# One 128-row product per pair of modes: a zero-padded block-diagonal stationary in place of two 64-row products

## The chip, the core and the metric

The kernel runs on one core of a Trainium2 chip. The metric is the device time of one execution in microseconds (us). Each kernel was executed several times; a median and the single runs are given. The profile is taken from one of those executions, and its "span" is some 1.7 us shorter than the time of the same run, so spans are compared with spans and times with times. Short names: PE is the matrix engine, PEld its weight loads, DVE the vector engine, ACT the scalar engine, POOL the engine that issues the weight loads from memory, DMA the sixteen transfer engines of the core.

## The reference

Attention features first (left out here), then a mixing of frequencies: for each of 64 modes, an eight-row matrix of complex numbers is multiplied with its own complex 512 x 512 matrix.

```python
# x: (8, 576, 512) out of a linear attention; w_r, w_i: (64, 512, 512) fp32; w_ch: (512, 512)
X  = np.fft.rfft(x, axis=1)
Xr, Xi = np.real(X[:, :64]), np.imag(X[:, :64])
Yr = einsum('bmd,mde->bme', Xr, w_r) - einsum('bmd,mde->bme', Xi, w_i)
Yi = einsum('bmd,mde->bme', Xr, w_i) + einsum('bmd,mde->bme', Xi, w_r)
y  = np.fft.irfft(Yr + 1j * Yi, n=576, axis=1)      # modes from 64 on are zero
u  = x + y
out = u + np.maximum(u @ w_ch, 0.0)
```

`w_r` and `w_i` together are 134 MB in fp32 and are used once. They are most of what the core reads.

## The kernel before

The modes are handled in 31 pairs and one last pair, whose second mode has a path of its own. The weights of a pair lie in one tile of 128 partitions: 64 for the even mode, 64 for the odd one, 16 blocks of 512 columns (`NDW = 16`). `NDC` is 4, `B` is 8, `D` is 512. A pair uses 32 products with 64 rows each, into two PSUM banks; four of them at a time stand side by side in four column tiles of the array, so a bank holds four partial results below one another. A copy brings a bank to SBUF, and four matmuls with a 0/1 table (`pick_sb`) sum the four parts and turn the result. The cut below is shortened: the `pin(...)` calls, which keep the program order, are left out, and a two-branch `if` is written in one line.

```python
def product(P, kk, w, dc):                                   # one of 32 per pair
    c = dc % NDC * 32                                        # column tile
    n = 32 if dc < NDC else 2 * B
    rows = slice(0, 128) if last else HALVES[kk % 2]         # 64 rows: even or odd mode
    nc.tensor.matmul(P[c : c + n, :], xt_cols(dc, kk, n), w[rows, dc, :],
                     start=(dc < NDC), stop=(dc >= n_dc - NDC), tile_position=(rows.start, c), ...)

def evacuate(kk, P):                                         # one per mode
    st = ystage.tile([128, D], F16, tag="ystage", bufs=2, ...)
    nc.vector.tensor_copy(out=st, in_=P) if kk % 2 == 0 else nc.scalar.copy(out=st, in_=P)
    return st

def picks(kk, st):                                           # four per mode
    for ec in range(NDC):
        nc.tensor.matmul(yt_ps[:, ec, kk % 8, :], st[:, ec * 128 : ec * 128 + 128], pick_sb)

def mode_pair(p):
    w = w_get(p)                                             # issues the next load into the buffer that is free
    ...
    for dc in range(NDW):
        for P, kk in zip(Ps, kks):
            product(P, kk, w, dc)
    sts = [evacuate(kk, P) for P, kk in zip(Ps, kks)]
    work_slot(p, "mid")                                      # other work of the program, spread over the pairs
    for kk, st in zip(kks, sts):
        picks(kk, st)
    ...
    # (cut: copies of yt_ps, further work, filler matmuls)
```

## Time and profile before

| | before |
|---|---|
| time, three runs | 423.23, 423.29, 424.82 us; median 423.29 |
| profiled span | 420.7 us |
| instructions counted | 8570 |
| PE busy | 292.1 us (69%), 3714 matmuls and as many weight loads |
| DVE, ACT, POOL busy | 215.7, 163.5, 56.9 us |

A share of busy time tells little here: no compute engine is above 69%, but the row of the DMA engines stands at 9 tenths for nearly the whole span. How the rows are read is told in the prediction, which shows them. One part of the page it does not show is the list of DMA queues (columns: number and kind, packets, MB, share of the sixteen engines' time). Two of its lines carry no data at all. They matter later, so here they are for the kernel before:

```profile
q8 instruction: 29, 0.48, 0.4%
q14 instruction: 8, 0.07, 0.0%
```

These queues bring the engines their instructions. Each of the 29 packets of the first is about 0.48 MB / 29 = 16 KB.

### The profile page before, as it was taken

What the parts mean: (1) busy time and instruction counts of PE and PEld (TensorE: products, weight loads), DVE (VectorE), ACT (ScalarE), POOL (GpSimd) and SP (SyncE); (2) the same over time, 40 slices, a digit from 0 to 9 for tenths busy, and PEclk for the clock granted to TensorE, in tenths of its full rate; (3) what the DMA queues carried; (4) which work ended last, traced back from release to release, by engine and by line L of the source; (5) the groups of instructions that cost most, each with busy time, mean ns of one, the idle gap of its engine ahead of it and who ended that gap; (6) DMA issues with size and microseconds to landing.
All of it is one profiled execution on the core that took longest, in us unless ns stands there. A gap on an engine that the chain in (4) does not pass through costs nothing.

```text
span 420.7 us, 8570 instructions
## 1 busy us (share of the span) xinstructions
PE 292.1 (69%) x3714; PEld 162.7 (39%) x3714; DVE 215.7 (51%) x446; ACT 163.5 (39%) x269; POOL 56.9 (14%) x99
## 2 busy tenths in 40 slices
PE   1369997999617645444343686978789896999992
PEld 0257775877402322122122232433334332365420
DVE  4588899695203453354544433454335332422794
ACT  4677797854202102000000243444335351231782
POOL 4222224210101111111111111111111111130000
PEclk9999998589855555555555589899989896899997
DMA  8999999999999999999999999999999999997697
GB/s 219 211 212 216 210 217 209 226 217 209 225 213 224 211 210 221 218 209 221 217 210 221 217 206 223 220 206 221 221 206 221 222 206 220 223 204 154 234 395 320
DMA packets 16421, 93.24 MB, mean 222 GB/s; under 512 B 2048, under 2 KB 2944, under 8 KB 11968
## 3 DMA queue, kind: packets, MB, share of 16 engines
q0 software_dynamic: 12416, 81.47, 93.1%
q1 hardware_dynamic: 3968, 11.22, 7.1%
q8 instruction: 29, 0.48, 0.4%
q14 instruction: 8, 0.07, 0.0%
HBM read 163.93 MB, written 9.44 MB: 412 GB/s over the span
## 4 chain that ended last, share of the span: by engine, by line
DMA 64%; PE 22%; DVE 6%; issue 2%; POOL 2%; ACT 2%; DVEq 0%; POOLq 0%; ACTq 0%
DMA w<-in_moe_w_i_dram 51%; DMA pick_sb<-row_pick 8%; PE P L438 7%; DMA k<-in_k_dram 5%; PE acc L732 3%; PE acc L771 2%; PE kvp L259 2%; POOL w L119 2%; PE zl L421 1%; PE eps L673 1%; ACT ke L210 1%; DVE ys L448 1%; DVE x L295 1%; PE ya L650 1%; PE yt L456 1%
## 5 line engine op out<-in xcount | busy, mean ns | idle before, releaser
L438 PE MATMUL P<-w,xt_c 64*32 64x512 bf16 (+2 forms) x1000 | 51.0, 538 | 59.5 <-DMA w<-in_moe_w_i_dram 58.1
L448 DVE CAST ys<-P 128x512 f16<-128x512 f32 x32 | 22.1, 692 | 123.7 <-PE P L438 123.7
L450 ACT CAST ys<-P 128x512 f16<-128x512 f32 x31 | 18.1, 585 | 155.6 <-PE P L438 155.6
L119 POOL DMA_DIRECT2D w<-in_moe_w_r_dram x31 | 17.3, 557 | 247.4 <-PE P L438 97.4
L438 PEld LDWEIGHTS <-xt_c 64*32 64x32 bf16 (+2 forms) x1000 | 16.8, 128 | 79.9 <-DMA w<-in_moe_w_i_dram 43.4
L673 PE MATMUL eps<-wch,xTw 128*128 128x512 f16 x144 | 39.4, 400 | 0.0
L165 PEld LDWEIGHTS <-qT 64*128 64x128 f16 (+1 forms) x640 | 23.4, 124 | 31.6 <-issue 18.0
L259 PE MATMUL kvp<-vpad,ke 32*128 32x130 f16 x576 | 24.3, 261 | 9.0 <-ACT qT L246 6.1
L656 ACT CAST x16w<-x_main 128x512 f16<-128x512 f32 x32 | 19.7, 618 | 23.6 <-DVE x_main L654 22.5
L654 DVE TENSOR_TENSOR x_main<-ya,x_main 128x512 f32<-128x512 f32 x32 | 22.0, 689 | 13.4 <-PE ya L650 13.3
L259 PEld LDWEIGHTS <-ke 32*128 32x128 f16 x576 | 22.2, 115 | 10.7 <-issue 8.2
L165 PE MATMUL nw<-kv,qT 64*128 64x65 f16 (+1 forms) x320 | 19.0, 240 | 9.5 <-DVE x_tail L617 4.3
L681 ACT CAST E<-eps 128x512 f16<-128x512 f32 (+1 forms) x40 | 21.2, 540 | 8.0 <-PE eps L673 8.0
L456 PE MATMUL yt<-pick_sb,ys 128*128 128x16 f16 x252 | 11.7, 174 | 17.2 <-DMA pick_sb<-row_pick 10.6
L295 DVE TENSOR_TENSOR x<-num,rd 128x512 f16<-128x512 f32 x32 | 22.1, 692 | 1.1
L239 PE MATMUL qTp<-id,qe 128*128 128x128 f16 x144 | 14.1, 277 | 11.3 <-DVE qe L223 9.4
L210 ACT ACTIVATE qe<-q 128x1152 f16<-128x1152 f16 (+1 forms) x16 | 17.9, 1157 | 8.1 <-DMA q<-in_q_dram 8.0
L165 PE MATMUL num<-kv,qT 64*128 64x65 f16 (+1 forms) x320 | 16.4, 218 | 5.5 <-DVE x L295 3.2
L456 PEld LDWEIGHTS <-ys 128*128 128x128 f16 x252 | 9.6, 101 | 27.3 <-DVE ys L448 15.0
L246 ACT COPY qT<-qTp 128x1152 f16<-128x1152 f16 x16 | 19.6, 1292 | 0.8 <-PE qTp L239 0.6
L210 ACT ACTIVATE ke<-k 128x1152 f16<-128x1152 f16 x16 | 17.7, 1153 | 5.5 <-DMA k<-in_k_dram 4.0
L421 PE MATMUL zl<-wch,id 128*128 128x512 f16 x72 | 19.6, 409 | 0.0
(113 smaller groups left out, 476.5 us busy)
## 6 DMA issues: line engine op xcount, KB each, us to landing
w<-in_moe_w_r_dram POOLq DMA_DIRECT2D x31, 1024.0 KB, 13.0
w<-in_moe_w_i_dram POOLq DMA_DIRECT2D x31, 1024.0 KB, 17.4
out_dram<-x_main SPq DMA_DIRECT2D x10, 512.0 KB, 4.0
k<-in_k_dram POOLq DMA_DIRECT2D x8, 576.0 KB, 12.9
v<-in_v_dram POOLq DMA_DIRECT2D x8, 576.0 KB, 14.5
q<-in_q_dram POOLq DMA_DIRECT2D x7, 576.0 KB, 12.7
out_dram<-x_main SPq DMA_DIRECT2D x2, 1024.0 KB, 5.0
q<-in_q_dram SPq DMA_DIRECT2D x2, 576.0 KB, 4.4
```

Of the source, the lines that this page charges most:

```text
L119: nc.gpsimd.dma_start(out=w_in[p][half::2], in_=two.rearrange("g (r dc) e -> (g r) dc e", dc=NDW))
L165: mm = nc.tensor.matmul(num[hpo][orow, c0 : c0 + 65], qT[rows, hpp, h2, cols], kv_sb[rows, hpp, h2, :])
L210: pin(nc.scalar.activation(out=ev[:, c], in_=heads(nm, b, c), func=AF.Exp))
L259: nc.tensor.matmul(kv_ps[:, h2, 0:130], phi["k", b][r0 : r0 + 32, j // NJ, j % NJ].rearrange("p o d -> p (o d)"), vp[r0 : r0 + 32, :, j, 0 ...
L295: nc.vector.tensor_tensor(out=dst.rearrange("p (o c d) -> p o c d", o=2, c=4), in0=nv[:, :, :, 0:64], in1=rden.unsqueeze(3).broadcast_to([ ...
L421: pin(nc.tensor.matmul(last_ps[0], id16, wch16[:, 0, :]))
L438: nc.tensor.matmul(P[c : c + n, :], xt_cols(dc, kk, n), w[rows, dc, :], start=(dc < NDC), stop=(dc >= n_dc - NDC), tile_position=(rows.sta ...
L448: pin(nc.vector.tensor_copy(out=st, in_=P))
L456: nc.tensor.matmul(yt_ps[:, ec, kk % 8, :], st[:, ec * 128 : ec * 128 + 128], pick_sb)
L654: pin(nc.vector.tensor_tensor(out=x, in0=acc, in1=x, op=ALU.add))
L673: nc.tensor.matmul(e_ps, xT[:, c, :], wch16[:, c, :], start=(c == 0), stop=(c == NDC - 1))
L681: pin(nc.scalar.copy(out=dst, in_=e_ps[:, cols]))
```

## The change

The intent is to let one product do both modes of a pair. The stationary operand becomes 128 rows by 32 columns: rows 0 to 63 hold the even mode's numbers in columns 0 to 15 and zeros elsewhere, rows 64 to 127 the odd mode's in columns 16 to 31. One PSUM bank then holds both modes, one copy brings it out, and four sums with a 32-column table do for both. In return, DVE must write that stationary for every pair.

```diff
-    def product(P, kk, w, dc):
+    def product(P, x, n, w, dc, n_dc):
...
-                P[c : c + n, :], xt_cols(dc, kk, n), w[rows, dc, :],
-                start=(dc < NDC), stop=(dc >= n_dc - NDC), tile_position=(rows.start, c),
+                P[c : c + n, :], x, w[:, dc, :],
+                start=(dc < NDC), stop=(dc >= n_dc - NDC), tile_position=(0, c),
...
+    def set_diagonal(p):
+        for h in range(2):
+            src = xt_v[HALVES[h], :, :, :, p].rearrange("p c t b -> p c (t b)")
+            pin(nc.vector.tensor_copy(out=xz[p % 2][HALVES[h], :, h, :], in_=src))
...
         for dc in range(NDW):
-            for P, kk in zip(Ps, kks):
-                product(P, kk, w, dc)
-        sts = [evacuate(kk, P) for P, kk in zip(Ps, kks)]
+            product(P, xz[p % 2][:, dc].rearrange("p h n -> p (h n)"), 32, w, dc, NDW)
+        if p + 1 < LAST:
+            set_diagonal(p + 1)
+        st = evacuate(p, P)
         work_slot(p, "mid")
-        for kk, st in zip(kks, sts):
-            picks(kk, st)
+        picks(2 * p, st, 2)
...
+    xz = [ystage.tile([128, NDW, 2, 2 * B], BF16, name=f"xz{i}") for i in range(2)]
+    for i in range(2):
+        nc.vector.memset(xz[i], 0.0)
+    set_diagonal(0)
```

Cut from the diff: the table of 32 in place of 16 columns, and the same calls in the last pair.

More of the change, by code (lines that the diff above doesn't have):

```diff
@@ L34, in _dft_consts @@
     inv[:, 1, :] = -np.sin(ang) * scale[:, None]
-    pick = np.zeros((128, 16), dtype=np.float16)
+    pick = np.zeros((128, 32), dtype=np.float16)
     for quad in range(4):
-        for c in range(16):
+        for c in range(32):
             pick[quad * 32 + c, c] = 1.0
@@ L82 @@
     fwd_sb = const.tile([128, 5, 2 * NM], F16, name="fwd_sb")
-    pick_sb = const.tile([128, 16], F16, name="pick_sb")
+    pick_sb = const.tile([128, 32], F16, name="pick_sb")
     wch16 = const.tile([128, NDC, D], F16, name="wch16")
@@ L92, in xt_cols @@
     def xt_cols(dc: int, kk: int, n: int):
-        if kk // 2 == LAST:
-            part, dc = slice(0, 128), (dc // NDC * 2 + kk % 2) * NDC + dc % NDC
-        else:
-            part = HALVES[kk % 2]
+        dc = (dc // NDC * 2 + kk % 2) * NDC + dc % NDC
         c0 = dc * XDC + kk // 2
-        return xt_c[part, c0 : c0 + (n - 1) * NMP + 1 : NMP]
+        return xt_c[:, c0 : c0 + (n - 1) * NMP + 1 : NMP]
     QW = 4 * NJ * NP
@@ L429, in work_slot, with product @@
                 work.pop(0)()
-    def product(P, kk: int, w, dc: int):
-        last = kk // 2 == LAST
-        n_dc = NDL if last else NDW
+    def product(P, x, n: int, w, dc: int, n_dc: int):
         c = dc % NDC * 32
-        n = 32 if dc < NDC else 2 * B
-        rows = slice(0, 128) if last else HALVES[kk % 2]
         pin(
             nc.tensor.matmul(
-                P[c : c + n, :], xt_cols(dc, kk, n), w[rows, dc, :],
-                start=(dc < NDC), stop=(dc >= n_dc - NDC), tile_position=(rows.start, c),
+                P[c : c + n, :], x, w[:, dc, :],
+                start=(dc < NDC), stop=(dc >= n_dc - NDC), tile_position=(0, c),
                 skip_group_check=True,
@@ L443, in product, with set_diagonal, evacuate @@
         )
-    def evacuate(kk: int, P):
-        st = ystage.tile([128, D], F16, tag="ystage", bufs=2, name=f"ys{kk}")
-        if kk % 2 == 0:
+    def set_diagonal(p: int):
+        for h in range(2):
+            src = xt_v[HALVES[h], :, :, :, p].rearrange("p c t b -> p c (t b)")
+            pin(nc.vector.tensor_copy(out=xz[p % 2][HALVES[h], :, h, :], in_=src))
+    def evacuate(p: int, P):
+        st = ystage.tile([128, D], F16, tag="ystage", bufs=2, name=f"ys{p}")
+        if p % 2 == 0:
             pin(nc.vector.tensor_copy(out=st, in_=P))
@@ L451, in evacuate, with picks @@
         return st
-    def picks(kk: int, st):
+    def picks(kk: int, st, n: int):
         for ec in range(NDC):
@@ L456, in picks @@
                 nc.tensor.matmul(
-                    yt_ps[:, ec, kk % 8, :], st[:, ec * 128 : ec * 128 + 128], pick_sb
+                    yt_ps[:, ec, kk % 8 : kk % 8 + n, :].rearrange("p m n -> p (m n)"),
+                    st[:, ec * 128 : ec * 128 + 128],
+                    pick_sb[:, 0 : n * 2 * B],
                 )
@@ L463, in mode_pair @@
         w = w_get(p)
-        kks = (2 * p, 2 * p + 1)
         if p % 4 == 0:
             yt_ps = psW.tile([128, NDC, 8, 2 * B], F32, tag="yt", bufs=1, name=f"yt{p // 4}")
-        Ps = [psW.tile([128, D], F32, tag="P", bufs=2, name=f"P{kk}") for kk in kks]
+        P = psW.tile([128, D], F32, tag="P", bufs=2, name=f"P{p}")
         for dc in range(NDW):
-            for P, kk in zip(Ps, kks):
-                product(P, kk, w, dc)
-        sts = [evacuate(kk, P) for P, kk in zip(Ps, kks)]
+            product(P, xz[p % 2][:, dc].rearrange("p h n -> p (h n)"), 32, w, dc, NDW)
+        if p + 1 < LAST:
+            set_diagonal(p + 1)
+        st = evacuate(p, P)
         work_slot(p, "mid")
-        for kk, st in zip(kks, sts):
-            picks(kk, st)
+        picks(2 * p, st, 2)
         if p % 4 == 3:
-            if kks[1] < NF:
-                pin(nc.vector.tensor_copy(out=YE_T[:, :, kks[1] - 7 : kks[1] + 1, :], in_=yt_ps))
+            kk = 2 * p + 1
+            if kk < NF:
+                pin(nc.vector.tensor_copy(out=YE_T[:, :, kk - 7 : kk + 1, :], in_=yt_ps))
             else:
-                g = (kks[1] - NF) // NL + 1
+                g = (kk - NF) // NL + 1
                 pin(nc.vector.tensor_copy(out=YL[:, :, :, g, :], in_=mode_rows(yt_ps)))
@@ L489, in last_pair @@
         for dc in range(NDL):
-            product(P, kk, w, dc)
+            n = 32 if dc < NDC else 2 * B
+            product(P, xt_cols(dc, kk, n), n, w, dc, NDL)
         st = evacuate(kk, P)
         work_slot(LAST, "mid")
-        picks(kk, st)
+        picks(kk, st, 1)
         pin(nc.vector.tensor_copy(out=Y8[:, :, 0 : NL - 1, :], in_=yt_ps[:, :, 0 : NL - 1, :]))
```

## The prediction

> **What bounds the kernel now.** I read the summary first, then the chain of waits, then busy time by stage, then single pairs in the timeline.
>
> The summary has a row that never leaves 9 between the start and the last tenth of the span: the DMA engines. The rate under it is flat from slice to slice.
>
> ```profile
> span 420.7 us, 8570 instructions
> ...
> DMA  8999999999999999999999999999999999997697
> ...
> HBM read 163.93 MB, written 9.44 MB: 412 GB/s over the span
> ## 4 chain that ended last, share of the span: by engine, by line
> DMA 64%; PE 22%; DVE 6%; issue 2%; POOL 2%; ACT 2%; DVEq 0%; POOLq 0%; ACTq 0%
> ```
>
> PE is 69% busy, DVE 51%, ACT 39%. The chain that ended last is DMA for 64% of the span, 51 points of it the weights (`w<-in_moe_w_i_dram`). The table by stage (columns: stretch, its length, busy time and instructions of PE, PEld, DVE, ACT and POOL, granted clock, DMA share, GB/s) shows the same rate whatever the compute engines do:
>
> ```profile
> 9.00:60.00 51.00, 38.24 (x610) 31.29 (x610) 41.12 (x78) 39.24 (x51) 11.52 (x16) 1.00 1.11 216
> ...
> 140.00:232.00 92.00, 40.35 (x678) 20.35 (x679) 43.20 (x143) 7.27 (x15) 10.49 (x20) 0.50 1.01 216
> 232.00:362.00 130.00, 104.89 (x985) 46.47 (x984) 53.57 (x101) 49.72 (x90) 14.13 (x26) 0.87 1.02 216
> 362.00:389.00 27.00, 25.95 (x280) 14.92 (x279) 9.55 (x17) 8.19 (x14) 4.90 (x9) 1.00 0.90 188
> 389.00:392.50 3.50, 2.92 (x23) 1.92 (x24) 1.76 (x4) 1.59 (x4) 0.57 (x1) 1.00 0.00 0
> ```
>
> PE is busy 40 of 92 us in one stage and 105 of 130 in the next, and the DMA moves 216 GB/s (as bf16; twice that is read as fp32) in both. All input bytes land by about 389 us; 163.93 MB in 389 us is 421 GB/s. What follows (389 to 420.7 us) is the tail: the last inverse transform and the stores. **So the time is some 389 us of loading plus some 31.7 us of tail**, and the change touches neither directly.
>
> It could touch the loading if PE released weight buffers so late that the DMA ran dry. The timeline of one pair (start, duration, engine, idle before it and its releaser) and the DMA issues tell how far off that is:
>
> ```profile
> 192.93 1.95 PE L438 MATMUL P<-w,xt_c 64*32 64x512 bf16 x32 [4.77 <-DMA w<-in_moe_w_i_dram]
> ...
> 194.80 0.47 PEld L165 LDWEIGHTS <-qT 64*128 64x128 f16 x16 [0.85 <-issue]
> ```
>
> ```profile
> w<-in_moe_w_i_dram POOLq DMA_DIRECT2D x31, 1024.0 KB, 17.4
> ```
>
> PE waited 4.77 us for these weights; PE came early, not late. A pair is 2 x 1024 KB of bf16, so at 216 GB/s it needs 2.097 MB / 216 GB/s = 9.7 us. The second load of a pair lands a median 17.4 us after issue, so at issue there was about 17.4 - 9.7 = 7.7 us of earlier work queued. **PE would have to release a buffer some 7 us later (less latency, say 5) before the DMA noticed; releasing it earlier gains nothing.** The smallest such figure on the chain is the load issued at 140.16 us after the early pairs, 13.5 us to landing, so about 3.8 us queued.
>
> **What the Trainium skill says.**
> - "TensorE: Matmul & The Clock Gate", Part 3 (packing small matmuls): matmuls in different row and column tiles of the array run at the same time, and a short contraction takes as long as a full one. The trace agrees: alone at half clock one 512-column matmul streams 512 / 1.2 GHz = 427 ns (that page's back-to-back formula), and 32 of them (2 row halves x 4 column tiles) take 1.87 us from first start to the next instruction on PE, which is four rounds of 427 ns plus 0.16, not 32 nor 16 rounds.
> - Same page, Part 1: the PE clock has a half and a full state set by recent activity. The trace shows 0.50 until about 245 us and mostly 1.00 after it, where the kernel issues filler matmuls.
> - "Perfetto Trace Analysis", Identifying Performance Opportunities: improving a kernel means improving the most-contended engine. Here that is the DMA, which the change leaves alone.
> - "DMA: Bandwidth & Descriptors", Bandwidth, Measured: 425 GB/s for a 16 MB transfer by one core alone. The 421 worked out above agrees, so I see no headroom in the loading.
>
> **The change part by part.**
>
> *Products.* 31 pairs x 32 matmuls of 64 rows become 31 x 16 of 128 rows (the last pair is already 128 rows: 8 before and after). So 1000 matmuls become 504. Not half the time: before, the two 64-row halves shared the array, four rounds of eight; after, four rounds of four. The old kernel holds the new shape in its last pair, `128*32 128x512 bf16 x8`: started at 385.25, the next PE instruction at 385.85, 0.60 us for two rounds at full clock. Two more rounds at 512 / 2.4 GHz = 0.21 us make 1.03 us for 16. The 32 of pair 30 took 379.16 to 380.19 = 1.03 us. **Saving: 0.0 us per pair**, both clocks.
>
> *Copies out of PSUM.* The rows of section 5:
>
> ```profile
> L448 DVE CAST ys<-P 128x512 f16<-128x512 f32 x32 | 22.1, 692 | 123.7 <-PE P L438 123.7
> L450 ACT CAST ys<-P 128x512 f16<-128x512 f32 x31 | 18.1, 585 | 155.6 <-PE P L438 155.6
> L119 POOL DMA_DIRECT2D w<-in_moe_w_r_dram x31 | 17.3, 557 | 247.4 <-PE P L438 97.4
> ```
>
> Each copy waits for products, and the weight issues (third row) wait for PE, which reads the weights, not for the copies. Even pairs now copy on DVE, odd ones on ACT: DVE 32 to 17 (-15 x 0.692 = -10.4 us), ACT 31 to 15 (-16 x 0.585 = -9.4 us). The two copies of a pair ran side by side, so a pair's latency stays 0.69, or 0.59 when ACT does it.
>
> *Sums (picks).* 252 become 31 x 4 + 4 = 128, each with 32 columns. Eight took 0.38 us at half clock, spaced by the weight loads at about 0.29 / 8 = 36 ns, so four fewer save about 0.15 us per pair, **4.5 us of PE time in all**.
>
> *Added: the diagonal.* Two DVE copies per pair, 64 partitions x 256 bf16, read with a 64-byte step, and two memsets. No row has this shape; small SBUF copies show 182 ns for 32 elements and 200 ns for 64, about 0.56 ns an element. At that to 1.04 ns an element (my estimate's upper end, from the 692 - 182 over 480 more elements of the PSUM copy) one takes 0.31 to 0.42 us; 62 of them, **19 to 26 us of DVE**. Net DVE is +9 to +16 us, about 225 to 232 us busy of 420. In program order on DVE the copy for pair p+1 stands before the copy-out of pair p and waits only for products of pair p-1, so it runs while PE waits for weights. On the path only for pair 0: two memsets and two copies, 1 to 1.3 us, before products that started at 112.21. Its sums then wait until 124.75 for the small pick table, the last in the load queue, and the weight load it releases (114.51) has about 10 us of queue ahead. Hidden.
>
> Sum of what lies beside the DMA: PE -4.5, ACT -9.4, DVE +9 to +16 us. **Sum on the path: 0.** The one place where PE meets the last bytes is 389.01 us, where it waited 0.17 us for them; the 0.15 us saved in pair 30 only lengthens that wait. The tail has no changed instruction.
>
> **The rivals.**
> 1. *PE work in the late stage was the bound.* For: the chain passes PE from 235 to 246 and from 351 to 362 us. Against: through both the DMA holds 214 to 216 GB/s. If it were so, 0.15 x 16 pairs = 2.4 us faster, still under 1%.
> 2. *Products get twice as fast* (PE bound by instruction issue, 1 us saved per pair). Against: four rounds fit both clocks. Even then the pairs wait for weights: 0.
> 3. *Less PE activity drops the clock to half after 245 us.* PE is busy 85 of 105 us there at clock 0.95; at half clock it would need more than 9.7 us a pair and starve the DMA, some 2 us x 10 pairs = +20 us. For: the page already shows it at half around 312 and 352. Against: array time per pair is unchanged, and the fillers stay. I give it 2%.
> 4. *DVE becomes the bound in 140 to 232 us.* It is busy 43 of 92; 9 pairs x 0.75 more stays far under.
>
> **Range and chances.** The three runs before spread from 423.23 to 424.82, a median of 423.29. With zero on the path I predict 423.2; the range 421.8 to 425.0 is that spread plus about 1 us of gain for rival 1. Within 2% is 414.8 to 431.8: 97%. Faster 1%, slower 2% (rival 3).
>
> **What would show it.** In the new profile: the DMA row at 9 to slice 36; the y_last stage still at about 389; 16 product matmuls in about 1.03 us at full and 1.87 at half clock; PE busy a few us lower with about 620 fewer matmuls; about 495 DVE instructions with DVE busy up; the wait of PE for `w` longer, not shorter. I am wrong if the last weights land off 389 by more than 2 us, if a hole appears in the DMA row, or if the clock falls after 245 us.

## The result, and the profile after

The changed kernel took 421.63 us (median of six runs, 421.39 to 422.74), the kernel before on the same chip 423.65 us (six runs, 423.12 to 424.82). The ratio is 0.9953, with a 95% interval from 0.9935 to 0.9971. Ratios are always computed in this way: the mean time of one kernel's fast runs over that of the other's fast runs of the same rounds, so a ratio is not quite that of the medians quoted beside it. The interval lies below 1, so the kernel is faster by a little, and 421.63 lies just under the low end of the predicted range, 421.8.

Four repeats, each with five rounds beside the kernel before on the same chip, gave 422.19, 421.33, 421.92 and 421.98 us against 422.93, 422.54, 422.80 and 423.06. The ratios are 0.9979, 0.9986, 0.9981 and 0.9980. Three of their four intervals just include 1 (upper ends 1.0005, 1.0002 and 1.0003; the first ends at 0.9997), but all four ratios lie on the same side. So the gain is nearer 0.2% than 0.5%, some 0.8 us on the mean and about 1 us between undisturbed runs. In the first comparison the kernel before ran slower than later (median 423.65, in the four repeats 422.54 to 423.06).

The summary after, with the shares of the chain that ended last in its final line, shows the same picture as before:

```profile
span 419.9 us, 7345 instructions
...
PE 289.4 (69%) x3094; PEld 156.2 (37%) x3094; DVE 228.3 (54%) x495; ACT 153.7 (37%) x253; POOL 57.0 (14%) x99
...
DMA  8999999999999999999999999999999999997698
...
DMA 62%; PE 24%; DVE 5%; issue 3%; ACT 3%; POOL 2%; DVEq 0%; ACTq 0%; POOLq 0%
```

The DMA row has no hole, and 1225 instructions are gone. The two instruction queues, on which the explanation will rest, now read

```profile
q8 instruction: 24, 0.39, 0.3%
q14 instruction: 9, 0.07, 0.0%
```

that is, five packets fewer in queue 8 than before. The table by stage (its columns are those told in the prediction) gives the same rate in the two long stages:

```profile
140.00:232.00 92.00, 38.40 (x486) 17.73 (x489) 46.13 (x155) 4.25 (x10) 9.78 (x18) 0.50 1.02 216
232.00:362.00 130.00, 104.90 (x715) 44.31 (x709) 58.90 (x122) 45.97 (x84) 14.76 (x28) 0.87 1.02 216
```

The costliest groups, first of the kernel before, one line the prediction told in words, then of the changed kernel (columns: line, engine, operation, operands, count, busy us and mean ns of one, idle time before and what ended it):

```profile
L438 PE MATMUL P<-w,xt_c 64*32 64x512 bf16 (+2 forms) x1000 | 51.0, 538 | 59.5 <-DMA w<-in_moe_w_i_dram 58.1
```

```profile
L431 PE MATMUL P<-w,xz 128*32 128x512 bf16 x496 | 49.4, 538 | 65.1 <-DMA w<-in_moe_w_i_dram 62.6
L448 ACT CAST ys<-P 128x512 f16<-128x512 f32 x15 | 8.8, 585 | 127.9 <-PE P L431 127.9
...
L446 DVE CAST ys<-P 128x512 f16<-128x512 f32 x17 | 11.8, 692 | 56.8 <-PE P L431 56.8
...
L441 DVE COPY xz<-xt_c 64x256 bf16<-64x256 bf16 x62 | 23.1, 372 | 11.2 <-PE P L431 10.4
```

Half as many products keep PE busy for the same 50 us, and PE now waits longer for weights (62.6 against 58.1 us): it has not become the bound. A single pair near the end of the timeline shows the same, 16 products from 378.29 until the next instruction at 379.26:

```profile
378.29 1.05 PE L431 MATMUL P<-w,xz 128*32 128x512 bf16 x16 [0.76 <-DMA w<-in_moe_w_i_dram]
379.26 0.69 PE L713 MATMUL yp<-id,YL 128*64 128x128 f16 x8
```

So where did the microsecond go? The chain of waits narrows it (start, duration, what ran or was waited for). Before:

```profile
124.75 0.36 PE yt L456 x8
...
362.86 26.11 DMA w<-in_moe_w_i_dram x2
388.97 0.04 issue
389.01 0.30 PE y_last L501 x4
```

And after:

```profile
124.75 0.27 PE yt L454 x4
...
386.94 1.17 PE y_last L502 x28
388.11 0.04 issue
388.15 0.30 PE y_last L502 x4
```

In both kernels the first sums, which wait for the small pick table, start at 124.75 us. In both, the tail from the last four `y_last` matmuls to the end takes 31.7 us (420.7 - 389.01 and 419.9 - 388.15). The difference, 0.86 us, arises between 124.75 and 389 us, while the DMA streams weights.

**A finer measure.** The trace has a record of each DMA packet. For the rest of this document, "the loading" is the time from the end of the pick table's last packet to the end of the last weight packet. It was worked out from these records for every profiled run: 264.45 us before, 263.57 us after. It leaves out what PE does with the last weights.

### The profile page after: what moved, and what is told of

It is laid out like the page before. It is cut to its first block, busy times and chain, and to the rows that moved or that the text cites. A ratio compares the mean times of both kernels' runs of the same rounds, so it can differ in the third digit from the quotient of the medians.

```text
span 419.9 us, 7345 instructions
## 1 busy us (share of the span) xinstructions
PE 289.4 (69%) x3094; PEld 156.2 (37%) x3094; DVE 228.3 (54%) x495; ACT 153.7 (37%) x253; POOL 57.0 (14%) x99
## 4 chain that ended last, share of the span: by engine, by line
DMA 62%; PE 24%; DVE 5%; issue 3%; ACT 3%; POOL 2%; DVEq 0%; ACTq 0%; POOLq 0%
DMA w<-in_moe_w_i_dram 49%; DMA pick_sb<-row_pick 8%; PE P L431 8%; DMA k<-in_k_dram 5%; PE acc L737 3%; PE acc L776 2%; PE kvp L256 2%; PE zl L418 2%; POOL w L116 2%; PE eps L678 2%; ACT ke L207 1%; DVE x L292 1%; PE yt L454 1%; ACT ys L448 1%; DVE ke L220 1%
## 5 line engine op out<-in xcount | busy, mean ns | idle before, releaser
L431 PE MATMUL P<-w,xz 128*32 128x512 bf16 x496 | 49.4, 538 | 65.1 <-DMA w<-in_moe_w_i_dram 62.6
L448 ACT CAST ys<-P 128x512 f16<-128x512 f32 x15 | 8.8, 585 | 127.9 <-PE P L431 127.9
L431 PEld LDWEIGHTS <-xz 128*32 128x32 bf16 x496 | 13.4, 116 | 86.8 <-DMA w<-in_moe_w_i_dram 55.4
L446 DVE CAST ys<-P 128x512 f16<-128x512 f32 x17 | 11.8, 692 | 56.8 <-PE P L431 56.8
L678 PE MATMUL eps<-wch,xTw 128*128 128x512 f16 x144 | 40.9, 412 | 0.0
L441 DVE COPY xz<-xt_c 64x256 bf16<-64x256 bf16 x62 | 23.1, 372 | 11.2 <-PE P L431 10.4
L622 DVE TENSOR_TENSOR x_main<-nw,rd 128x256 f32<-128x256 f32 x32 | 11.2, 415 | 17.3 <-PE nw L162 17.3
L454 PE MATMUL yt<-pick_sb,ys 128*128 128x32 f16 (+1 forms) x128 | 8.7, 185 | 16.0 <-DMA pick_sb<-row_pick 9.8
```

Source lines behind the costliest of these rows:

```text
L431: nc.tensor.matmul(P[c : c + n, :], x, w[:, dc, :], start=(dc < NDC), stop=(dc >= n_dc - NDC), tile_position=(0, c), skip_group_check=True,)
L441: pin(nc.vector.tensor_copy(out=xz[p % 2][HALVES[h], :, h, :], in_=src))
L678: nc.tensor.matmul(e_ps, xT[:, c, :], wch16[:, c, :], start=(c == 0), stop=(c == NDC - 1))
```

## The experiments

Three theories were set against each other.

- **A, instructions beside weights.** PE has fewer instructions. They too come over the DMA, in the packets of queue 8, and 24 remain of 29. Less of that traffic lets the weights in sooner.
- **B, earlier release.** PE finishes a pair earlier, so the buffer is free and the next load is issued earlier. The load of pair 7 was issued at 139.62 us before and at 138.72 after.
- **C, fewer copies.** DVE and ACT make 31 fewer copies of a PSUM bank to SBUF, and that leaves more room for the DMA's writes.

The runs came in five jobs, each with its own runs of the kernel before on the same chip; the medians of these were 422.93, 422.88, 422.54, 422.80 and 423.06 us. A small diff stands for each kernel, against the changed kernel unless it says otherwise. The times of single runs scatter by more than the microsecond in question, so a median decides little by itself; the length of the loading is the finer measure. The expectations call the runs by short names: e2 is the first try with empty instructions, e3 the later release, e6 the PE instructions put back, e7 the 4096 SyncE instructions, e10 twice the dose of e6, e17 the kernel before with fewer instructions, e18 the moved packet.

### The changed kernel again (four runs)

Nothing was edited. These runs are the controls of their jobs.

> The changed kernel itself, as a control on the same chip as the next three. Theories of where its 2 us come from: A (instruction fetch): PE's program is 1240 instructions shorter, and PE's instructions come through the same DMA engines as the weights, in packets of 16 KB that each hold one engine for about 0.95 us; A, B and C alike expect 0.993 to 0.998 of the kernel before here, and the profile 24 instead of 29 packets on the instruction queue. B (earlier release of the weight buffers), C (fewer copies on DVE and ACT beside the loading). If it is noise: 0.999 to 1.001.

> The changed kernel once more, as the control for the next three on their chip: 24 packets of PE instructions, last weights at 388.1 to 388.4 us, 0.995 to 0.998 of the kernel before.

> The changed kernel, control for the next three: 24 packets of PE instructions, last weights at 387.9 to 388.4 us, fastest run 421.2 to 421.6 us.

> The changed kernel, control for e18: fastest run 421.2 to 421.6 us.

The times are given above. The loading took 263.33, 263.34, 263.56 and 263.50 us. The six runs of each fall into two groups, for instance 421.24, 421.30, 421.54 and then 422.30, 422.48, 424.29. The profile of the third repeat happened to fall on its slowest run, the 424.29. Its loading was as usual, but the clock row (PEclk, tenths of the full clock in 40 slices) dips to 5 late, and PE reached the last products late, so that all 32 ran as one chain:

```profile
390.08 0.92 PE y_last L502 x32
```

In that run, what was slow was PE near the end, not the loading.

### More PE instructions that do nothing, first try

```diff
+        for _ in range(40):
+            pin(nc.tensor.nop(nofuse=True))       # in every pair
```

> The changed kernel with 40 empty instructions on PE ahead of each of the 31 pairs: 1240 in all, so that PE's program is as long as before, while products, copies and sums stay as changed. A: the gain is lost, ratio to before 0.998 to 1.002, about 29 packets on the instruction queue. B and C: the gain stays, 0.993 to 0.997.

The time was 421.55 us (0.9976 [0.9951, 1.0000]). But the page counts 7345 instructions and 24 packets in queue 8, exactly as without the edit: the empty instructions never reached the chip. This run tests nothing. It serves as one more repeat; its loading took 263.47 us.

### Later release of the weights

```diff
+        for i in range(4):                        # zeros times the last weight blocks, added to P
+            pin(nc.tensor.matmul(P, wzero, w[:, NDW - 4 + i, :], start=False, stop=(i == 3), ...))
```

> The changed kernel with four more full-width matmuls per pair that read the pair's weights against a zero stationary (result unchanged): the buffer is released about 1.7 us later at half clock and 0.9 us later at full clock, with 248 more PE instructions (one packet). A: stays at 0.994 to 0.998. B: later release costs at least what the change gained, ratio 1.000 or above. C: stays at 0.993 to 0.997.

424.82 us (422.80 to 426.90), ratio 1.0042 [1.0015, 1.0069]. Pair 7's load was issued at 140.76 us, 2.0 us later than in the changed kernel, and the loading took 266.68 us, 3 us more. Lateness far smaller than the prediction's "some 7 us" (and than its smallest figure, 3.8 us) already goes with a longer loading, and between 141.1 and 143.7 us engines of the DMA were without a packet for 7.2 us, summed over the sixteen. Whether the lateness or the additional PE work does it, this run alone does not tell.

### The same additional work without reading the weights, and half of it

```diff
-            nc.tensor.matmul(P, wzero, w[:, NDW - 4 + i, :], ...)
+            nc.tensor.matmul(P, wzero, fwd_sb[:, 0:4, :].rearrange("p c n -> p (c n)"), ...)   # first kernel
+            nc.tensor.matmul(P, wzero, w[:, NDW - 2 + i, :], ...)                              # second: two, not four
```

> Control for the late release (e3), which cost 2.6 us: the same four full-width zero matmuls per pair in the same place on PE, but reading a constant tile instead of the pair's weights, so that the weight buffer is released by the products as in the changed kernel. If e3 was slow by its late release (B): back to within 0.2% of the changed kernel. If by its extra PE work, later copies or clock: as slow as e3, about 424.5 us.

> e3 with two instead of four extra matmuls on the weights: release about 0.85 us later at half clock. If the cost of a late release is a threshold (engines of the DMA that run ahead meet an empty queue): less than half of e3's 2.6 us, 0.2 to 1.0 us over the changed kernel. If proportional: 1.3 us. If a late release is hidden as the prediction had it: 0.

The first gave 424.24 us (421.70 to 426.59), ratio 1.0021 [0.9987, 1.0054]. It was meant as a control, but failed as one: the additional matmuls slowed PE's catching up on the first five pairs, so pair 7's load was issued at 143.32 us, later still. Its loading took 266.46 us. The second gave 421.80 us (421.46 to 425.68), ratio 0.9990 [0.9959, 1.0020]; its profile fell on its slowest run, in which pair 7's load was issued only at 143.55 us. In the profiled runs of the three, a pair-7 load issued 2 to 5 us later goes with a loading 3 to 4 us longer, and in all three some DMA engines are without a packet for moments in the 10 to 30 us after 124.7 us. They do not show that a load issued 0.9 us *earlier*, as by the change, gains anything. In the changed kernel no engine of the sixteen was without a packet from 125 to 380 us. In the kernel before there were two small holes, one engine for 0.4 us at 141.4 us and for 0.15 us at 248.4; the earlier release closed them. That they cost nothing is shown further down, by a kernel that has the first of them and the short loading all the same.

### Copies put back

```diff
-        if p % 2 == 0: vector copy to st
-        else:          scalar copy to st
+        one, other = (st, st2) if p % 2 == 0 else (st2, st)
+        pin(nc.vector.tensor_copy(out=one, in_=P))
+        pin(nc.scalar.copy(out=other, in_=P))     # the second copy is thrown away
```

> The changed kernel with each pair's sums copied out twice, on DVE and on ACT (the second copy goes to a spare tile): the 31 copies that the change took away come back, PE's program stays short. A and B: stays at 0.993 to 0.997. C: back to 0.998 to 1.002.

421.79 us (421.51 to 423.24), ratio 0.9972 [0.9954, 0.9990]. The groups show that the copies were really made:

```profile
L448 ACT CAST yt<-P 128x512 f16<-128x512 f32 x17 | 10.0, 586 | 88.6 <-DVE ys L447 55.4
...
L447 DVE CAST yt<-P 128x512 f16<-128x512 f32 x15 | 10.4, 692 | 50.6 <-PE P L431 50.6
```

That is as many copies as before the change, and the gain in time is still there. The loading took 263.93 us, 0.4 to 0.6 us longer than in the controls, so this run alone would leave a part of the gain to theory C. The kernel with fewer instructions below, which has all the old copies and loads in 263.37 us, does not: with it theory C falls.

### PE instructions put back

Matmuls with one column do little, but each is two instructions, the weight load and the product. 620 of them bring the stream back to the old 3714 matmuls.

```diff
+        for _ in range(200 if p == 0 else 0):      # while the pick table is awaited
+            pin(nc.tensor.matmul(yt_ps[0:32, 0, 2 * p % 8, 0:1], id16[:, 0:32], id16[:, 0:1]))
+        for _ in range(42 if 5 <= p < 15 else 0):  # ahead of a pair, while PE waits for weights
+            pin(nc.tensor.matmul(...))             # the same
```

> The empty instructions of the second run (e2) never reached the chip: its instruction queue still shows 24 packets, so it tested nothing. This kernel adds 1240 real PE instructions (620 one-column matmuls with their 32-column weight loads) to the changed kernel, where PE waits anyway: 200 while it waits for the pick table, 42 ahead of each of pairs 5 to 14. A (instruction fetch beside the weights): 29 instead of 24 packets of 16 KB, weights finished 0.5 to 1.2 us later than in the changed kernel, time +0.2 to +0.3% over it. B (release of the buffers) and C (copies): no change to the changed kernel within 0.1%.

423.39 us (422.55 to 425.02), ratio 1.0010 [0.9986, 1.0033]. By the median the gain is gone. The queue has its old packets, and the last weights land late as before the change:

```profile
q8 instruction: 29, 0.48, 0.4%
...
389.13 0.30 PE y_last L514 x4
```

(The first line is from the page, the second from the chain.) The loading took 264.40 us. This line of the queue also confirms what it carries: 1240 additional PE instructions made five packets more, 248 each, or about 66 bytes an instruction. Because this edit delays a few pairs (pair 7's load was issued at 139.97 us), it was made again with all additions outside pairs 5 to 7 (305 at the table, 45 in each of pairs 8 to 14):

> e6 again (1240 PE instructions more), but placed only in the wait for the pick table (305 matmuls) and ahead of pairs 8 to 14 (45 each), so that no load of the early pairs is issued later. A: 29 packets, last weights 0.7 to 1.1 us later than in the control, fastest run about 422.5 us. B (e6 was slow by its delay at pair 5): as the control.

422.74 us (422.43 to 424.14), ratio 1.0003 [0.9987, 1.0020], 29 packets, loading 264.66 us. Its fastest run, 422.43, is that of the kernel before in this job (422.49), not that of the changed one (421.24). This run and the control of its job are the cleanest pair: in both, pair 7's load was issued early (138.60 and 138.80 us), both profiles fell on a slow run, and the DMA had no hole until 374 us and nearly the same one there (8.9 and 9.4 us summed over the engines). With five packets more, the loading is 264.66 us against 263.56.

### Twice the dose, the same PE time in few instructions, and SyncE instead

```diff
+        # first: 300 at the table and 130 in each of pairs 8 to 14, one column each: 2420 instructions
+        # second: about the same PE time in 75 matmuls of 512 columns: 150 instructions
+        for _ in range(8 if 8 <= p < 15 else 0):
+            pin(nc.tensor.matmul(P, id16, fwd_sb[:, 0:4, :].rearrange("p c n -> p (c n)"), ...))
+    # third and fourth: empty work on another engine, SyncE
+    for _ in range(1024):                          # fourth: 4096
+        pin(nc.sync.drain())
```

> The changed kernel with 2420 real PE instructions more (1210 one-column matmuls with their weight loads: 300 in the wait for the pick table, 130 ahead of each of pairs 8 to 14, where PE waits for weights), twice the dose of e6. A: 33 or 34 packets of PE instructions instead of 24, weights finished 1.1 to 2.2 us later than in the control, time 0.25 to 0.5% over it. If PE's instruction count does not matter: as the control.

> Control for e6 and e10: about the same PE time in the same waits, but as 75 long matmuls (19 and 7 x 8 of 512 columns, some 0.43 us each) instead of 1210 short ones, so 150 PE instructions more, one packet at most. A: 24 or 25 packets, weights and time as the control within 0.1%. If e6 was slow by its PE time: as slow as e10.

> A quarter of the dose of e7, which cost 8.3 us of loading for 32 packets of 8 KB that all took 0.322 us, as if all went through one DMA engine (32 x 0.322 = 10.3 us) and not over 16 (0.6 us). Here 1024 drains, 8 packets. If the most loaded DMA engine sets the end: 8 x 0.322 = 2.6 us on it, weights 1.0 to 2.6 us later than in the control. If the load spreads: 0.2 us.

> The changed kernel with 4096 extra instructions on SyncE (drains, behind its last early load), 256 KB of extra instruction stream on an engine that computes nothing. A: 16 to 32 more packets on an instruction queue, weights finished about 1 to 2 us later than in the changed kernel, time +0.2 to +0.5% over it. B and C: no change.

*Twice the dose:* 423.09 us (422.36 to 426.15), ratio 1.0027 [1.0002, 1.0053], 33 packets. The profile fell on a slow run with a loading of 267.91 us, and pairs were delayed, so its size says little about packets; the median is in the expected direction.

*The same PE time, few instructions:* 422.30 us (422.21 to 423.95), ratio 1.0002 [0.9990, 1.0015]. By its time this is a miss for theory A, under which it should have kept the gain. The loading kept it: 263.38 us, 25 packets of which 23 came before the last weights, and the last four products started early:

```profile
387.82 0.30 PE y_last L516 x4
```

The time was lost after that: 420.3 - 387.82 = 32.5 us of tail in place of 31.7. Its last PE packet came 24 us after the last weights, amid the output stores. So the times of the runs with added instructions do not decide between packets and PE time, since this one lost as much time without the packets; their loadings do.

*1024 empty SyncE instructions:* 422.54 us (421.46 to 424.09), ratio 1.0007 [0.9990, 1.0024]; eight more packets of queue 14. The loading was 263.33 us, that is, not longer; the median is nevertheless 1.2 us above the control of its job (421.33), and in the profile this lies after the last weights, 33.0 us to the end against 31.9. *4096 of them:* 430.41 us (428.93 to 431.46, five runs), ratio 1.0167 [1.0141, 1.0192]:

```profile
q14 instruction: 41, 0.34, 0.2%
...
382.19 14.21 DMA w<-in_moe_w_i_dram
396.44 0.30 PE y_last L502 x4
```

This is theory A in the large. 32 more packets of 8 KB, 0.26 MB among 82 MB, went with a loading 8.3 us longer than the 263.4 us of the controls. Nearly every one of these packets took 0.322 us. Spread over sixteen engines they would cost 32 x 0.322 / 16 = 0.64 us; all on one engine, 10.3 us. The weights are done when the most laden engine is done, so traffic that falls on one engine counts in full, less what that engine had to spare. Six of the eight packets of the smaller dose fell in the loading, 1.9 us, and cost nothing there, so it had at least that. The sum is not exact: from 219 us on, with the 4096, other engines had moments without a packet too (10 us summed over them) and many weight packets took longer, so part of the 8.3 us came about indirectly.

### Two packets, and the old kernel with fewer instructions

```diff
+        for _ in range(256 if p == 0 else 0):      # 512 instructions at the pick table: two packets
+            pin(nc.tensor.matmul(...))             # one column, as above
```

> The changed kernel with 512 PE instructions more (256 one-column matmuls in the wait for the pick table): 26 packets, some 25 of them before the last weights. If the most loaded of eight engines sets the end: one of them now carries four packets, last weights 0.7 to 1.1 us later, as with 29 packets. If the mean over the engines counts: 2 x 1.07 / 16 = 0.13 us later, not to be told from the control.

422.70 us (422.16 to 425.28), ratio 1.0003 [0.9980, 1.0027]. The median shows no gain any more, with two of the five packets back. The loading was 264.83 us, with the last weights at

```profile
389.27 0.30 PE y_last L508 x4
```

In this profile the loads of pairs 6 and 7 were also issued 2.6 us later than in the control of the job (129.79 and 141.35 us), and there were holes, the longest 1.3 us on one engine at 131.5 us, so part of its loading is due to that. How large a part is worked out after the table of loadings.

The opposite test takes the kernel *before* and thins its PE stream, with its copies, its sums and its stationary left alone. To do so it leaves out the middle half of every product sum: it computes something else. The comparison with the reference still passed, which only says that its tolerance is wide for a part that adds little to the output. Two full-width products with zeros make up for the PE time, so that the buffers are released when they used to be.

```diff
 # against the kernel before
-        for dc in range(NDW):
+        for dc in (*range(NDC), *range(NDW - NDC, NDW)):
...
+        for i, P in enumerate(Ps):
+            pin(nc.tensor.matmul(P, wzero, w[:, NDW - 2 + i, :], start=False, stop=True, ...))
```

> The kernel before with half of its products left out (the middle eight of the sixteen row blocks; the result is wrong on purpose) and two full-width zero matmuls on the pair's weights in their place, so that PE takes the same time and releases the buffer when it did, with 868 PE instructions fewer: 26 packets instead of 29. A by the mean: 0.2 us earlier. A by the most loaded engine: 25 packets before the last weights, still four on one engine, so the same as before or, if 24, about 1 us earlier. B and C (release and copies as before): the same as before within 0.1%.

420.60 us (five runs, 420.57 to 420.67), ratio 0.9944 [0.9932, 0.9955]. Pair 7's load was issued at 139.29 us, within 0.4 us of the kernel before; all old copies are there; only some 870 instructions are missing. From the page and the chain:

```profile
q8 instruction: 25, 0.41, 0.4%
...
387.25 0.92 PE y_last L507 x32
```

The loading took 263.37 us, as in the changed kernel. So the gain of the loading comes without the changed copies, without the diagonal and without an earlier release at pair 7. (Its very first load was issued at 111.17 us, 3.3 us before that of the kernel before; but two repeats of the changed kernel issued theirs only at 119.56 and 119.30 us and loaded in 263.34 and 263.50 us, so that does not matter.) It even has a hole like that of the kernel before, 0.3 us on one engine at 141.3 us. That leaves theory A. Its expectation had said "if 24, about 1 us earlier", and 24 of its 25 packets came before the last weights. PE did its last 32 products in one go, with no wait for weights in between: here PE itself had become the limit at that place. This kernel gained about 0.8 us more in the tail, 30.8 us from the start of the last `y_last` product (388.0 us) to the end against 31.6 in the kernel before (389.1 us), which theory A had not said.

### Is the tail due to a packet amid the stores?

In the changed kernel the last PE packet comes while the outputs are stored, in this last test it does not. 58 one-column matmuls move it.

```diff
+        for _ in range(58 if p == 0 else 0):
+            pin(nc.tensor.matmul(...))             # one column, as above
```

> The changed kernel with 116 more PE instructions (58 one-column matmuls in the wait for the pick table). In the changed kernel the last packet of PE instructions comes 13 us after the last weights, amid the stores; 116 instructions ahead of it move it to about 3 us after them, before the stores have filled the DMA, as in e17, and no further packet is needed. If a packet amid the stores lengthens the tail: 24 packets as before, tail 0.5 to 0.9 us shorter, fastest run about 420.6 us, though more instructions are run. If not: as the control, fastest run about 421.3 us.

422.11 us (421.25 to 422.85), ratio 0.9971 [0.9952, 0.9990]; its control was at 421.98 (0.9980). The packet did move: the last one now comes 2 us after the last weights, in the changed kernel 13 us after them. But the span was 419.5 us and the fastest run 421.25, as in the control (419.6 and 421.37), not 420.6. So the packet of PE is not what lengthens the tail. Two packets of queue 14 still fall late among the stores in it, 19 and 27 us after the last weights, as in the changed kernel (20 and 27). In the kernel before it is one of PE, 17 us after them; in the thinned kernel no instruction packet comes later than 8.2 us after them. Whether any packet there is enough was not tested, and the 0.8 us of the tail stay open.

### All loadings side by side

The number of packets is that of PE's queue that came before the last weights landed.

| kernel | PE packets | loading, us |
|---|---|---|
| changed kernel, first run and four repeats | 23 | 263.33 to 263.57 |
| no-ops (not executed), moved packet, long matmuls, 1024 SyncE | 23 | 263.33 to 263.47 |
| copies put back | 23 | 263.93 |
| kernel before, thinned | 24 | 263.37 |
| two packets put back | 25 | 264.83 |
| 620 matmuls put back | 27 | 264.40 |
| the same, cleaner | 28 | 264.66 |
| kernel before | 28 | 264.45 |

The runs with late releases (four, 266.5 to 267.9) and with 4096 SyncE instructions (271.70) are left out. Up to 24 packets the loading took 263.3 to 263.9 us, from 25 on 264.4 to 264.8. That looks like a step rather than a slope, though the runs with 25 and 27 packets had their pairs delayed as well. A packet of weights took 1.23 us, a PE packet of the same size 0.89 to 0.97, and with what the weight packet beside it lost about 1.1 us. Five of them spread evenly over sixteen engines would cost 5 x 1.1 / 16 = 0.34 us. The durations of PE's packets repeat with a period of eight (893, 949, 945, 935, 974, 974, 961, 892 ns, then 893, 948, 945 again), which suggests that they go round eight engines. Then 23 or 24 of them are three on the most laden one, and 25 to 28 are four: one packet more, about 1.1 us, which is the step.

The records do not name the engine, but it can be followed. During the loading, an engine's next 16 KB packet of weights starts within a few nanoseconds of a fixed moment, 19 ns before its last one ends, so these packets fall into sixteen chains. (Two chains whose times coincide can be mistaken for each other now and then.)

Between 135 and 366 us of the kernel before, PE's 15 packets delay eight of the sixteen chains in a strict round, each time the one that was hit eight packets earlier. From its packet of the pick table to its last 16 KB packet of weights, a chain without a PE packet takes 252.35 us, one with one packet 253.5, one with two 254.5 to 254.6. At the start the eight chains are already behind by the packets that came before: the pick table lands on most of the others at 121.6 to 122.3 us, on these at 122.8 to 124.3. In the kernel before, an engine on which it landed at 124.24 us gets two more packets and ends last, at 378.81 us. In the changed kernel those at 124.2 get one more and end at 377.73, and one at 123.37 gets two and ends last, at 377.96. That difference, 0.85 us, is within 0.03 us the difference of the loadings.

Seven of the eight engines without PE packets are done more than 3 us earlier. In the run with two packets put back, the engine that ends last (pick table at 124.13 us) has two packets where the controls have one, and took 254.94 us, so about 1.1 us of its longer loading is that packet and some 0.4 us are the holes. SyncE's added packets delay one single chain, one that PE's packets leave alone; with the 4096 it can be followed so until 249 us.

## Why the prediction was right or wrong, point by point

**Right: products, copies, sums, diagonal.** 16 products at full clock took 0.97 us from start to the next instruction (predicted 1.03), at half clock 1.83 us (1.87): four rounds before and after, so nothing was saved there. DVE went from 446 to 495 instructions and to 228.3 us (predicted 225 to 232); one diagonal copy took 372 ns (0.31 to 0.42 us), 62 of them 23.1 us (19 to 26). ACT lost 9.8 us (9.4). PE lost 2.7 us, not 4.5: the sums' own busy time fell by 3.0 us (11.7 to 8.7), since one with 32 columns takes 185 ns and one with 16 took 174, and other groups changed by one to two microseconds either way. The load after pair 0 was issued at 115.27 us in place of 114.51, 0.76 us later (1 to 1.3 was said), but in the repeats it was issued anywhere from 114.44 to 119.56 us, so this says little. Two readings in the prediction are off without consequence: the clock row does not stand at 0.50 "until about 245 us", since the prediction's own table has 1.00 from 9 to 60 us; and (692 - 182) / 480 is 1.06 ns an element, not 1.04.

**Right: the rivals stayed rivals.** The clock did not fall after 245 us, DVE did not become the bound, the products did not get faster, and PE waits longer for `w`, not shorter. The last weights landed 0.86 us earlier, within the 2 us that the prediction allowed.

**Wrong: "Sum on the path: 0."** The prediction says that the most-contended engine "is the DMA, which the change leaves alone", and of the loading and the tail that "the change touches neither directly". From 421 GB/s beside the 425 of the skill's page it concluded "no headroom in the loading". This is the step that failed: the change does touch the loading. The omitted term is the PE's own instruction stream, which shares the sixteen engines with the weights: 7428 instructions became 6188, 29 packets 24. Its size is the step in the table, 264.45 - 263.57 = 0.9 us in the first pair of profiles, 0.9 to 1.1 us against the repeats. The page had it: 8570 instructions and the line of queue 8 were on the first page read. At 0.4% of the engines' time it looked like nothing; it is nothing on average, and a packet in full, about 1.1 us, on the engine that ends last.

**Wrong in size: the slack.** The prediction let PE be "some 7 us later" before the DMA would notice, and 3.8 us at the smallest place. In the run with later release, 2.0 us at pair 7 went with a loading 3 us longer. This did not decide the outcome, because the change did not make releases late, but the argument "releasing it earlier gains nothing" stood on a slack that was not there: the prediction took the DMA as one queue, while its engines run 2 to 3 us apart (the pick table landed on them between 121.6 and 124.2 us), and one of them was without a packet for 0.4 us already in the kernel before. The statement held nevertheless, by luck as far as its reason goes: the thinned kernel kept the old release times and had the whole gain of the loading.

**Wrong in the range.** The low end was 421.8, "about 1 us of gain for rival 1". A gain of that size came, by another way, and put the first median at 421.63, 421.24 to 421.63 in the fastest runs of the five sets. No median came into the upper half of the range, to 425.0. The first comparison, 2.0 us between the medians, is about twice what the repeats showed.

**What the Trainium skill says on it.** "Runtime: NRT & Kernel Launch", section "Instruction fetch mechanics", says that instructions are fetched in blocks of 16 KiB by a DMA queue that the sequencer drives itself, and calls the cost of crossing such a block "mostly hidden". The traces agree on the block (16,384 bytes for PE) and on a queue of its own (queue 8). The page speaks of the engine that fetches. What other traffic pays is not in it, and here that was not hidden: the weights, which fill the DMA, gave way by about a microsecond. The prediction's first citation draws on two places: that tiles run at the same time is in Part 3 of "TensorE: Matmul & The Clock Gate", that a short contraction takes as long as a full one is in that page's closing table.

**What stays open.** Why PE's packets go round just eight of the engines was not asked. The 0.8 us gained in the tail of the thinned kernel, and about 1 us lost there in the ones with long matmuls and with 1024 SyncE instructions, are not explained. Slow runs of both kernels (to 424.9 us) were looked into in one profile only, where PE's clock fell near the end. No kernel that does the whole of the work beat the changed one.

## What to carry to other kernels

When the DMA is full from end to end, count everything that goes over it, instructions too: the page's queue list has them, and a change that looks neutral on every engine can still be worth a packet or two. Ask of such traffic what the most laden engine gets, not the mean. And where a change should be worth nothing, a gain of 0.2% needs repeats on one chip and a control that restores the one suspected thing, before it can be called real or explained.

## What the Trainium skill lacked or had wrong

- "Runtime: NRT & Kernel Launch", "Instruction fetch mechanics", calls the fetch "mostly hidden" and does not say what it costs other transfers. Beside a DMA that is full it was not hidden: the loading took 263.3 to 263.9 us with up to 24 PE packets and 264.4 to 264.8 us with 25 to 28.
- The same section gives blocks of 16 KiB. That is so for PE (24 to 29 packets of 16,384 bytes); SyncE's packets were 8,192 bytes, 128 instructions of 64 bytes each (4096 more instructions, 32 more packets); whether its block is one packet or two, the records do not tell.
- No page found tells over which DMA engines instructions come. PE's packets delay eight of the sixteen chains of weight packets in turn (15 packets in a strict round in the kernel before). SyncE's added packets, 0.322 us each, delay a single other one, and 32 of them went with a loading 8.3 us longer.
- No page found says that empty PE instructions can vanish: 40 in each of 31 pairs left the page at 7345 instructions and 24 packets.
